# The first two chunks of a fused attention and MoE kernel done in halves of the inner dimension, and batches 0 and 1 in groups of four heads

## The chip, the cores and the metric

The kernel runs on one core of one Trainium2 chip. The metric is the device time in microseconds of one execution; the time before is the median of three runs. The engines are called TensorE (PE), VectorE (DVE), ScalarE (ACT), GpSimd (POOL) and SyncE (SP, whose queue issues every transfer).

## The reference

Sparse attention over 8 batches, 8 heads, 576 positions and head size 64, then a gated two-layer network on all 8 x 576 = 4608 tokens of width 512, with an inner width of 2048.

```python
# attention, per batch and head
scores = q @ k.T / sqrt(D)
rel = pos[:, None] - pos[None, :]
mask_local   = (rel >= 0) & (rel < 32)                       # heads 0 to 3
mask_strided = (rel >= 0) & (pos[None, :] % 32 == pos[:, None] % 32)   # heads 4 to 7
attn = softmax(where(mask, scores, -1e9));  attn_out = attn @ v
# network
x = attn_out.transpose(0, 2, 1, 3).reshape(4608, 512)
h = x @ w_in                                                 # 512 x 2048
g = h * erf(softplus(h))
out = g @ w_out                                              # 2048 x 512
```

## The kernel before

**Attention.** Both masks are nearly block diagonal. The host lays the data out so that a block of 96 queries meets 128 keys (local heads), and a block of 126 (seven residues modulo 32, 18 positions each) meets its own 126 keys (strided heads). A batch has three steps `j` for each kind; a step has two blocks, the last strided one a single block of 72. Heads are taken in pairs `hp`: 0 and 1 are local, 2 and 3 strided.

Batches 0 and 1 use `piece(b, hp, j, ...)`, one head pair each, twelve to a batch. Its steps: load `qk` and `v`; scores on PE (line 302), where the two heads' queries stand side by side with zeros in the other head's 64 rows, so that the full 128 rows are used; the mask added on PE (line 312) as a product with the identity; a copy to SBUF on ACT (`mask`, line 320); the maximum over the keys on POOL (`maxi`, line 328); its subtraction, on PE for batch 0 (line 332, by a negated identity) and on DVE for batch 1 (line 337); the exponential on ACT (line 341); the product with v on PE (line 345), where a column of ones gives the sum; reciprocal and scaling (lines 356 to 370); a transpose on PE (line 376); and the split of the result into a high and a low part, on ACT (`xhi`) and DVE (`xlo`, line 399).

Batches 2 to 7 use `quad(b, loc, j, ...)`: four heads at once, six to a batch. Its scores (line 502) are *tiled*: products of 64 rows by 64 columns on quarters of the array, and only over the queries that a half of the keys can meet. It masks by a minimum on DVE, sums on POOL, and needs no transpose.

**Network.** Tokens are done in chunks of 384 (`CH`), twelve of them; three chunks cover two batches. Every chunk runs over 16 blocks `f` of 128 inner columns; chunk `c` and block `f` make tile `k = 16 c + f`. In `ftile`, the first product (called mm1, line 725) takes 12 matmuls of 384 columns: high by high, low by high and high by low parts, each over four blocks of 128 input columns. Then a chain of ACT and DVE steps follows (the gate, four ACT activations and four DVE steps, with the split into `ghi` and `glo`). The second product (mm2, line 788) takes nine matmuls of 512 columns and adds into three PSUM banks `o0` to `o2`, which are held through the chunk's 16 blocks; at the last block ACT copies them out (line 803) and SP stores them (line 806). mm1s keep the order in which the chunks are listed.

**Weights.** They come as 64-bit floats: 32 loads of 512 KB, 16 of `w_in` (four input blocks for each 512 inner columns) and 16 of `w_out` (one for each block `f`). Each tile of words is turned into a 32-bit float by three DVE steps (lines 677, 684, 690), then split into a high part on ACT (line 695) and a low part on DVE (line 698). The float is held in a buffer of the tag `ob` in between. An mm1 needs its four `w_in` tiles, an mm2 its `w_out` tile.

**Order.** No engine's order is left to the program text. Each step is given to `Plan` with an engine, a duration, a key and what it comes after; `Plan.order` lists the steps by their estimated start and, among those that can start together, by key. The keys come from the constants at the top: `PRO + SLOT * k` for a tile, `W1K`, `W1S`, `W2K`, `W2S` for the weights, `A0K`, `A1K` and so on for the attention. SP's list goes by the same rule, with an estimate of the bytes still under way. Buffers (`bufs`) turn in order; a step that takes a buffer waits for the last users of it. While PE has nothing to do before the first mm1 it runs short products without use (`warm`, line 916).

```python
bufs = {"qk": 2, "v": 3, "sm": 3, "mx": 2, "tt": 2, "ps": 2, "h": 3, "a": 2, "ghi": 2, "glo": 2,
        "ob": 3, "r": 2}
```

Here `qk` and `v` are the loaded inputs, `sm` the scores in SBUF, `ps` and `h` PSUM banks (attention and mm1), `a`, `ghi`, `glo` the gate's values.

Of the kernel before, what the change touches and what calls it, by code (L numbers as in the profile page):

```python
# [1 line left out]

# [16 lines left out]
P = 128  # L19
# [9 lines left out]
PRO = 76.3437  # L29
SLOT = 5.25715  # L30
MM2 = 22.7481
W1K = (13.4993, 31.795, 47.8243, 102.53)
W1S = (0.491029, 16.2659, 6.41024, 9.24383)
W2K = 83.5416
W2S = 5.03476
A0K = 10.4625
A0S = 0.93245
A0D = -13.616
A1K = 82.9925
A1S = 4.98533  # L40
A1D = -10.6234
QE = (17.2927, 2.07406, 29.6184, 2.17352)
QO = (2.25354, 2.66589)
QD = (-0.95595, 4.13274, 3.34602, 4.05869, -2.26784)
ASH = 5.35876
ADT = -0.840127
BACKLOG = 0.566644
FT = (-0.468742, -1.24448, 5.36844, 0.898218, 4.98625, -0.907662, 1.11257, 2.41173, -0.633009)
# [5 lines left out]
WL = 2 * 2 * QL + 2 * QL + 32  # L54
WS = 2 * 2 * QS + 2 * P
# [141 lines left out]
def attention_moe(  # L197
# [16 lines left out]
    wpool = ctx.enter_context(tc.tile_pool(name="wpool", bufs=1))  # L214
    ps_a = ctx.enter_context(tc.tile_pool(name="ps_a", bufs=1, space=PSUM))
# [10 lines left out]
    cap = cpool.tile([P, SW], BF16, name="cap")[:, : 2 * QL + QS]  # L226
# [9 lines left out]
    pools = {"apool": apool, "mpool": mpool, "wpool": wpool, "ps_a": ps_a, "ps_h": ps_h, "ps_o": ps_o}  # L236
# [23 lines left out]
    def piece(b, hp, j, key, dt, ring, pe_mask=False, pool_sub=False, early=False):  # L260

        loc = hp < 2
        nblk = 1 if (not loc and j == 2) else 2
        n = QL if loc else (QS if j < 2 else S - 4 * QS)
        units, cols = 2 * nblk, 2 * nblk * n
        pid = f"{b}_{hp}_{j}"
        qk = buf("apool", "qk", [P, WS], f"qk_{pid}")  # L270
        v = buf("apool", "v", [P, 2, 2, D + 1], f"v_{pid}")
        s = buf("ps_h", "h", [P, 512], f"s_{pid}") if early else buf("ps_a", "ps", [P, 512], f"s_{pid}")
        sm = buf("apool", "sm", [P, 512], f"sm_{pid}")
        mx = buf("apool", "mx", [P, 512], f"mx_{pid}")
        pav = buf("ps_o", f"o{hp % 2}", [P, 512], f"av_{pid}") if early else buf("ps_a", "ps", [P, 512], f"av_{pid}")
        xn_b = buf("apool", "tt", [P, 512], f"xn_{pid}")
        xn = View(xn_b, "p (u d) -> p u d", slice(0, 4 * D), u=4)
        rc = buf("apool", "r", [P, 16, 1], f"r_{pid}")
        pt = buf("ps_a", "ps", [P, 512], f"t_{pid}")

        def load_qk():
            if loc:
                yield nc.sync.dma_start(qk[:, :WL], qk_loc[b, hp, j])
            else:
                w = nblk * (2 * n + P)
                yield nc.sync.dma_start(qk[:, :w], qk_str[b, hp - 2, j, :, :w])

        def load_v():
            w = nblk * 2 * (D + 1)
            yield nc.sync.dma_start(v.tile.rearrange("p b h d -> p (b h d)")[:, :w], v_all[b, hp, j, :, :w])  # L290

        def masks():
            if loc:
                m = mask_l if j == 0 else mask_l[:, 1:2]
                return m.broadcast_to([P, 2, 2, n]), "p (b h q) -> p b h q", dict(b=2, h=2)
            return mask_s[:, :, :n].broadcast_to([P, units, n]), "p (u q) -> p u q", dict(u=units)

        def scores():
            k0, step = units * n, n if loc else P
            for blk in range(nblk):  # L300
                dst = s[:, blk * 2 * n : (blk + 1) * 2 * n]
                yield nc.tensor.matmul(  # L302
                    dst,
                    qk[:, k0 + blk * step : k0 + blk * step + P],
                    qk[:, blk * 2 * n : (blk + 1) * 2 * n],
                    start=blk == 0,
                    stop=not pe_mask,
                    skip_group_check=True,
                )
                if pe_mask:  # L310
                    m = (mask_l[:, int(j > 0 or blk > 0)] if loc else mask_s[:, :, :n]).broadcast_to([P, 2, n])
                    yield nc.tensor.matmul(
                        dst.rearrange("p (h q) -> p h q", h=2), ident_b, m, start=False, stop=True,
                        skip_group_check=True,
                    )

        def mask():
            src, dst = s[:, :cols], sm[:, :cols]
            if pe_mask:
                yield nc.scalar.copy(dst, src)  # L320
            else:
                m, r, sizes = masks()
                yield nc.vector.tensor_tensor(
                    out=dst.rearrange(r, **sizes), in0=src.rearrange(r, **sizes), in1=m, op=ALU.add
                )

        def maxi():
            yield nc.gpsimd.partition_all_reduce(mx[:, :cols], sm[:, :cols], P, ReduceOp.max)  # L328
# [10 lines left out]
        def exp():  # L339
            d = sm[:, :cols]  # L340
            yield nc.scalar.activation(d, s[:, :cols] if early else d, AF.Exp, scale=1.0 / D**0.5)
# [680 lines left out]
```

## Time and profile before

| | |
|---|---|
| Median of three runs | 936.76 us (936.0 to 940.07) |
| The profiled execution | 934.98 us, span 933.2 us |
| PE busy | 921.7 us (99%) |
| DVE busy | 678.5 us (73%) |
| ACT busy | 576.7 us (62%) |
| POOL busy | 323.3 us (35%) |
| Moved by DMA | 68.83 MB, mean 74 GB/s |
| Granted PE clock | 1.000 |

PE's 99% holds the `warm` products too, and a matmul's record runs on beyond the start of the next, so a busy PE is not always one at full speed. What PE does usefully is read from the distance between the starts of its products. The shares of the other engines are means over a start in which DVE and the transfers are full and a long middle in which they are not.

### The profile page before, as it was taken

To read this page: it belongs to the slowest core of one execution; us is meant where nothing else is said; L and a number is where in the kernel's file an instruction comes from. 1 tells how busy PE (TensorE), PEld (TensorE's weight loads), DVE (VectorE), ACT (ScalarE), POOL (GpSimd) and SP (SyncE) were. 2 spreads that over 40 slices of the span, in tenths; PEclk is the share of its full clock that TensorE was granted. 3 is DMA by queue.
4 is the path that set the end of the run, shared out by engine and by line. 5 is a ranking of instruction groups with operands and counts; after the bars stand their busy time and mean duration, and the time that the engine had idled before them with its cause. 6 is when DMAs were issued, how large, how long until landed. Compare 5 with 4: busy or idle time off the path is not lost.

```text
span 933.2 us, 16156 instructions
## 1 busy us (share of the span) xinstructions
PE 921.7 (99%) x5993; PEld 813.2 (87%) x5993; DVE 678.5 (73%) x1539; ACT 576.7 (62%) x1283; POOL 323.3 (35%) x160
## 2 busy tenths in 40 slices
PE   7999999999999999999999999999999999999998
PEld 6888898888888888888888888889888888999997
DVE  6999998677777777766867777775777777555553
ACT  4776677556566656656656656655655666655654
POOL 3443104525263444513535543342525353000000
PEclk9999999999999999999999999999999999999999
DMA  8997202111212113102112111211211210000000
GB/s 286 310 317 255 60 22 80 39 46 59 78 51 80 43 54 100 46 12 78 59 48 92 60 48 52 80 39 35 91 47 50 80 48 4 34 1 0 34 1 35
DMA packets 37663, 68.83 MB, mean 74 GB/s; under 512 B 4176, under 2 KB 18640, under 8 KB 37584
## 3 DMA queue, kind: packets, MB, share of 16 engines
q1 hardware_dynamic: 37584, 67.80, 22.5%
q8 instruction: 47, 0.77, 0.4%
q14 instruction: 32, 0.26, 0.1%
HBM read 58.34 MB, written 9.44 MB: 73 GB/s over the span
## 4 chain that ended last, share of the span: by engine, by line
PE 92%; DVE 6%; DMA 1%; ACT 0%; issue 0%; SPq 0%
PE o L788 43%; PE h L725 41%; PE ps L592 3%; PE ps L502 2%; DVE w L684 1%; DVE w L690 1%; PE s L302 1%; DVE w L677 1%; DVE a L730 1%; DVE pair L698 1%; DMA qk<-qk_str 1%; DMA words<-w_in 1%; PE ps L490 0%; PE warm L916 0%; DVE xlo L399 0%; PE ps L302 0%
## 5 line engine op out<-in xcount | busy, mean ns | idle before, releaser
L788 PE MATMUL o<-pair,ghi 128*128 128x512 f32 x1152 | 364.5, 398 | 0.0
L733 ACT ACTIVATE a<-a 128x384 f32<-128x384 f32 x576 | 292.4, 522 | 95.5 <-DVE a L730 87.6
L730 DVE SCALAR_TENSOR_TENSOR a<-a,h 128x384 f32<-128x384 f32 x384 | 210.5, 549 | 163.9 <-ACT a L733 161.5
L725 PE MATMUL h<-xhi,pair 128*128 128x384 f32 x1536 | 299.5, 337 | 1.5 <-DVE glo L760 1.4
L725 PEld LDWEIGHTS h<-xhi,pair 128*128 128x128 f32 x1536 | 270.0, 188 | 10.7 <-DVE glo L760 2.7
L788 PEld LDWEIGHTS o<-pair,ghi 128*128 128x128 f32 x1152 | 209.4, 188 | 42.5 <-issue 1.5
L788 PE MATMUL o<-pair,glo 128*128 128x512 f32 x576 | 224.9, 390 | 0.0
L528 POOL PARTITION_ALL_REDUCE mx<-sm x66 | 100.1, 1560 | 352.1 <-DVE sm L520 343.3
L548 POOL PARTITION_ALL_REDUCE su<-sm x66 | 181.8, 2798 | 42.4 <-ACT sm L542 42.4
L733 ACT ACTIVATE a<-h 128x384 f32<-128x384 f32 x192 | 94.3, 491 | 141.4 <-PE h L725 140.5
L725 PE MATMUL h<-xlo,pair 128*128 128x384 f32 x768 | 164.5, 336 | 0.0
L754 DVE TENSOR_TENSOR h<-a,h 128x384 f32<-128x384 f32 x192 | 106.7, 556 | 42.3 <-ACT a L733 42.3
L725 PEld LDWEIGHTS h<-xlo,pair 128*128 128x128 f32 x768 | 135.9, 188 | 0.0
L788 PEld LDWEIGHTS o<-pair,glo 128*128 128x128 f32 x576 | 108.1, 188 | 23.6
L757 ACT CAST ghi<-h 128x384 fp32r<-128x384 f32 x192 | 90.8, 473 | 57.2 <-PE o L788 55.6
L760 DVE TENSOR_TENSOR glo<-h,ghi 128x384 fp32r<-128x384 f32 x192 | 105.2, 548 | 18.3 <-ACT ghi L757 15.3
L328 POOL PARTITION_ALL_REDUCE mx<-sm x24 | 41.5, 1734 | 63.1 <-ACT sm L320 56.8
L542 ACT ACTIVATE sm<-sm 128x384 f32<-128x384 f32 (+2 forms) x66 | 36.3, 554 | 18.6 <-DVE sm L535 17.6
L535 DVE TENSOR_TENSOR sm<-sm,mx 128x384 f32<-128x384 f32 (+2 forms) x66 | 39.8, 613 | 0.2
L520 DVE TENSOR_TENSOR sm<-ps,cap 128x384 f32<-128x384 f32 (+2 forms) x66 | 37.0, 585 | 0.0
L592 PEld LDWEIGHTS ps<-sm,v 128*64 128x64 f32 x528 | 24.6, 136 | 9.3 <-issue 6.5
L592 PE MATMUL ps<-sm,v 128*64 128x96 f32 (+2 forms) x528 | 31.7, 260 | 0.0
(59 smaller groups left out, 531.6 us busy)
## 6 DMA issues: line engine op xcount, KB each, us to landing
qk<-qk_loc SPq DMA_DIRECT2D x48, 304.0 KB, 3.3
qk<-qk_str SPq DMA_DIRECT2D x32, 380.0 KB, 3.6
v<-v_all SPq DMA_DIRECT2D x80, 130.0 KB, 2.2
out<-ob SPq DMA_DIRECT2D x36, 256.0 KB, 2.1
words<-w_in SPq DMA_DIRECT2D x16, 512.0 KB, 5.0
words<-w_out SPq DMA_DIRECT2D x16, 512.0 KB, 5.3
qk<-qk_str SPq DMA_DIRECT2D x16, 136.0 KB, 2.5
v<-v_all SPq DMA_DIRECT2D x16, 65.0 KB, 1.9
```

The lines of the kernel that those rows point to most:

```text
L328: yield nc.gpsimd.partition_all_reduce(mx[:, :cols], sm[:, :cols], P, ReduceOp.max)
L528: yield nc.gpsimd.partition_all_reduce(mx[k][:, :cols], sm[k][:, :cols], P, ReduceOp.max)
L535: yield nc.vector.tensor_tensor(out=d, in0=d, in1=mx[k][:, :cols], op=ALU.subtract)
L548: yield nc.gpsimd.partition_all_reduce(su[k][:, :cols], sm[k][:, :cols], P, ReduceOp.add)
L592: yield nc.tensor.matmul(px[h * D : (h + 1) * D, c0 : c0 + n], v[i][:, blk, h, :D], sm[bank][:, c : c + n], start=True, stop=True,)
L725: yield nc.tensor.matmul(ph[:, :CH], win[4 * s + cc][:, w, fs], x[cc][:, c0 : c0 + CH], start=(i == 0), stop=(i == len(terms) - 1))
L730: yield nc.vector.scalar_tensor_tensor(out=out, in0=in0, scalar=scalar, in1=in1, op0=op0, op1=op1)
L733: yield nc.scalar.activation(dst, src, func, bias=bias[i], scale=scale)
L754: yield nc.vector.tensor_tensor(out=ph[:, :CH], in0=a.tile, in1=ph[:, :CH], op=ALU.mult)
L757: yield nc.scalar.copy(ghi.tile, ph[:, :CH])
L760: yield nc.vector.tensor_tensor(out=glo.tile, in0=ph[:, :CH], in1=ghi.tile.bitcast(F32), op=ALU.subtract)
L788: yield nc.tensor.matmul(po.tile, g[:, ts], wout[f][:, w], start=(f == 0 and i == 0), stop=(f == NFC - 1 and i == 2),)
```

## The change

1. **Halves.** The list of chunks begins with chunk 0 over blocks 0 to 7, chunk 1 over blocks 0 to 7, chunk 0 over blocks 8 to 15, chunk 1 over blocks 8 to 15; from chunk 2 on it is as before. `ftile` gets a position `pos` in the list for its key, and the bounds `fs0` and `fs1` of its half. After a first half ACT copies the three banks out and SP stores them in DRAM (`keep`); before the end of the second half SP fetches them again (`fetch`, after all the `keep`s, the last weight and the joins of the chunk before), and DVE adds them to the banks (`join`) in place of ACT's copy.
2. **Groups.** `piece` is replaced by `head(b, loc, j, ...)`, four heads at once, six to a batch. Scores are tiled as in `quad`, with the mask still added on PE, once for each of two banks; each group's transposes go to one bank of `h`. The order within batches 0 and 1 is changed (`pairs`).
3. **Layout.** Both kinds of group now load all four heads by one transfer each for `qk` and `v`, and queries are stored without the zero halves (only the single block of 72 keeps them).
4. **Buffers and keys.** `v` 3 to 2 (of twice the size), `sm` 3 to 4, `ob` 3 to 2, `r` 2 to 3, `qk` 2 of twice the size. Every weight, every group of batches 0 and 1 and every quad has a key of its own.

```diff
-W1K = (13.4993, 31.795, 47.8243, 102.53)
-W1S = (0.491029, 16.2659, 6.41024, 9.24383)
-W2K = 83.5416
-W2S = 5.03476
+WK = (4.91144, 11.7736, 23.138, 24.5684, 81.8744, 38.4492, 69.5594, 67.3198, 63.8053, 87.1793, 23.8467, 61.9943, 34.3175, 127.093, 128.211, 116.829, 48.1787, 88.0229, 98.8806, 108.272, 109.35, 101.869, 119.148, 122.481, 143.689, 141.299, 147.526, 158.814, 180.44, 185.601, 167.447, 190.663)
+LD = (-3.85602, -21.1748, -3.28922)
+HK = (-0.530228, 7.20494, 8.53691, 33.1626, 35.9049, 38.4686, 41.9683, 60.4056, 62.9357, 79.7229, 107.532, 105.476)
...
-WL = 2 * 2 * QL + 2 * QL + 32
-WS = 2 * 2 * QS + 2 * P
+WL = 4 * QL + 32
+WS = 2 * QS + 2 * P
+WE = 2 * (S - 4 * QS) + P
...
-    bufs = {"qk": 2, "v": 3, "sm": 3, "mx": 2, "tt": 2, "ps": 2, "h": 3, "a": 2, "ghi": 2, "glo": 2,
-            "ob": 3, "r": 2}
+    bufs = {"qk": 2, "v": 2, "sm": 4, "mx": 2, "tt": 2, "ps": 2, "h": 3, "a": 2, "ghi": 2, "glo": 2,
+            "ob": 2, "r": 3}
...
+    def loads(g, key):
+        lq = plan.add("sp", P * 8 * g.wq / 3.6e5, key - LD[0], g.load_qk, new=[g.qk])
+        lv = plan.add("sp", P * 8 * g.wv / 3.6e5, key - LD[1], g.load_v, new=[g.v])
+        return lq, lv
+
+    def head(b, loc, j, key, dt, early, bank):
...
+        def scores():
+            yield from g.scores()
+            for k in range(nbank):
+                r, z, m = g.masks(k, mask_l, mask_s)
+                yield nc.tensor.matmul(
+                    s[k][:, :cols].rearrange(r, **z), ident_b, m, start=False, stop=True, skip_group_check=True
+                )
...
-            if f == NFC - 1:
-                ob = buf("mpool", "ob", [P, DM], f"ob{t}_{c}")
+            if f == fs1:
+                near = t == NTT - 1 and (c < 2 or c == NCHUNK - 1)
+                ob = buf("apool", "tt", [P, DM], f"ob{t}_{c}_{f}") if near else buf("mpool", "ob", [P, DM], f"ob{t}_{c}_{f}")
...
+                def join(po=po, ob=ob):
+                    yield nc.vector.tensor_tensor(out=ob.tile, in0=po.tile, in1=ob.tile, op=ALU.add)
...
+                if fs1 < NFC - 1:
+                    part[c, t] = buf("dpool", f"part{c}{t}", [P, DM], f"part{c}{t}")
+                    o = add("act", act(DM, 0.06), ke, evac, [o], [ob], [po])
+                    kept[c, t] = add("sp", d_io, ke + 0.1, keep, [o], [part[c, t]], [ob])
+                    continue
+                if fs0:
+                    o_f = add("sp", d_io, ke - PF, fetch, [*kept.values(), w2[-1], *joined[:c * NTT]], [ob], [part[c, t]])
+                    o = add("dve", dve(DM), ke, join, [o, o_f], [], [ob, po])
+                    joined.append(o)
...
+        if b == 1:
+            return [(True, 0), (False, 0), (False, 1), (False, 2), (True, 1), (True, 2)]
...
+        if b == 0:
+            return [(True, 0), (True, 1), (False, 0), (False, 1), (False, 2), (True, 2)]
...
+            if c < 2:
+                chunk(c, 0, NFC // 2)
+                if c == 1:
+                    chunk(0, NFC // 2, NFC)
+                    chunk(1, NFC // 2, NFC)
+            else:
+                chunk(c, 0, NFC)
```

More of the change, by code (lines that the diff above doesn't have):

```diff
@@ L1 @@
 from contextlib import ExitStack
+from types import SimpleNamespace
 import concourse.bass as bass
@@ new lines, in scores @@
+        def scores():
+            if nblk == 1:
+                for i in range(2):
+                    c = i * wq
+                    yield nc.tensor.matmul(
+                        s[0][:, 2 * i * n : 2 * (i + 1) * n], qk[:, c + 2 * n : c + 2 * n + P], qk[:, c : c + 2 * n],
+                        start=i == 0, stop=True, skip_group_check=True,
+                    )
+                return
+            used = set()
+            for i in range(2):
+                for blk in range(2):
+                    cq = i * wq + blk * n
+                    ck = i * wq + 2 * n + blk * (n if loc else P)
+                    for part in range(2):
+                        for h in range(2):
+                            rows, cols_k = slice(h * D, (h + 1) * D), slice(part * 64, (part + 1) * 64)
+                            bank, c = place(i, blk, h)
+                            q0, q1 = meet[part]
+                            yield nc.tensor.matmul(
+                                s[bank][cols_k, c + q0 : c + q1],
+                                qk[rows, ck + part * 64 : ck + (part + 1) * 64],
+                                qk[rows, cq + q0 : cq + q1],
+                                start=(bank, part) not in used,
+                                stop=True, skip_group_check=True,
+                            )
+                            used.add((bank, part))
@@ L701, in weight @@
         if wide:
-            op = add("sp", P * 8 * n / 3.6e5, key - 8.0, load, new=[words])
+            op = add("sp", P * 8 * n / 3.6e5, key - LD[2], load, new=[words])
             op = add("dve", dve(n, 0.5), key, bits0, [op], [w], [words])
@@ L789, in mm2 @@
                         po.tile, g[:, ts], wout[f][:, w],
-                        start=(f == 0 and i == 0), stop=(f == NFC - 1 and i == 2),
+                        start=(f == fs0 and i == 0), stop=(f == fs1 and i == 2),
                     )
             o = add(
-                "pe", 0.682, v0 + MM2 * SLOT + 0.2 * t, mm2, [o_l] + ready[1] + ([order_o[t]] if f else []),
-                [po] if f == 0 else [], [ghi, glo] + ([] if f == 0 else [po]),
+                "pe", 0.682, v0 + MM2 * SLOT + 0.2 * t, mm2, [o_l] + ready[1] + ([order_o[t]] if f > fs0 else []),
+                [po] if f == fs0 else [], [ghi, glo] + ([] if f == fs0 else [po]),
             )
@@ L854, in attention_moe @@
             rows, sl = slice(c * P, (c + 1) * P), slice(f, f + SW)
-            op, pair = weight(i, w_in, rows, sl, W1K[i // 4] + W1S[i // 4] * (i % 4))
+            op, pair = weight(i, w_in, rows, sl, WK[i])
             w1.append(op)
```

543 lines of the change are left out of this document (226 added, 317 removed).

## The prediction

> **What bounds the kernel now.** I read the page's slices first, then a table of stages, then TensorE's (PE's) own timeline, and last the chain that ended last. VectorE's (DVE's) row of the 40 slices (23.3 us each, tenths) shows that the first six slices are another kernel than the rest:
>
> ```profile
> DVE  6999998677777777766867777775777777555553
> ```
>
> The table of stages says it closer. Columns after the window: its length, then busy us and instructions of PE, PE's weight loads, DVE, ScalarE (ACT) and POOL, then PE's granted clock, DMA share, GB/s:
>
> ```profile
> 0.00:43.00 43.00, 37.99 (x262) 29.50 (x263) 32.68 (x79) 27.18 (x81) 19.72 (x16) 1.00 0.89 292
> 43.00:60.00 17.00, 15.57 (x101) 14.42 (x100) 17.00 (x38) 13.42 (x35) 3.60 (x3) 1.00 0.92 334
> 60.00:90.00 30.00, 29.25 (x181) 24.79 (x181) 29.85 (x75) 20.74 (x46) 12.93 (x6) 1.00 0.87 290
> 90.00:103.00 13.00, 12.38 (x71) 9.89 (x70) 13.00 (x30) 7.88 (x20) 4.22 (x3) 1.00 0.28 75
> 103.00:140.00 37.00, 37.00 (x226) 33.30 (x227) 37.00 (x81) 24.83 (x54) 1.25 (x1) 1.00 0.11 34
> 140.00:900.00 760.00, 760.00 (x5018) 675.40 (x5017) 535.09 (x1217) 465.91 (x1017) 281.62 (x132) 1.00 0.16 51
> ```
>
> From 103 us to the end PE has no gap, and its work there is fixed; time can only be won before. To 90 us the DMA stream runs near 300 GB/s, and from 43 to 140 us DVE is full. The fillers ("warm", line 916) have their own table of stages, first row below; PE's timeline gives the milestones (start, length, the wait in brackets):
>
> ```profile
> 0.00:50.00 50.00, 11.23 (x73) 1.00 0.90 303
> 42.88 1.64 PE L725 MATMUL h<-xhi,pair 128*128 128x384 f32 x8
> 48.00 0.49 PE L302 MATMUL ps<-qk 128*128 128x192 f32 x2
> 53.77 1.66 PE L725 MATMUL h<-xhi,pair 128*128 128x384 f32 x8 [1.40 <-DVE glo L760]
> 90.28 1.65 PE L725 MATMUL h<-xhi,pair 128*128 128x384 f32 x8
> 112.79 0.23 PE L376 MATMUL ps<-ident,xn 72*128 72x72 f32 x1
> ```
>
> The first MoE product (mm1 of tile 0) starts at T0 = 42.88; before it PE does batch 0 and 11.2 us of fillers. The ninth mm1 starts at T1 = 90.28, so eight tiles took 47.4 us. At full speed two tiles cost 4.17 + 4.08 us, by these chain rows:
>
> ```profile
> 190.69 4.17 PE h L725 x24
> 194.85 4.08 PE o L788 x18
> ```
>
> Eight tiles are 33 us at that rate, and not all their second products (mm2) were issued by T1. The rest is batch 1's attention on PE and stalls. Batch 1's scores begin at 48.00, its last transpose is at 112.79.
>
> **The change, part by part.**
>
> *Halves.* Chunk 0 runs hidden blocks 0 to 7, then chunk 1 the same, then chunk 0 and chunk 1 blocks 8 to 15. No matmul is added or dropped: 192 tiles stay. What moves is the deadline of 16 of the 32 weight tiles, by eight positions or more, and that of batch 1: chunk 1 now starts at position 8, not 16. A weight tile costs DVE four instructions:
>
> ```profile
> L684 DVE SCALAR_TENSOR_TENSOR w<-words,w 128x512 uint32<-128x512 uint32 x32 | 23.6, 737 | 0.1
> L690 DVE SCALAR_TENSOR_TENSOR w<-words,w 128x512 uint32<-128x512 uint32 x32 | 22.7, 710 | 0.1
> L698 DVE TENSOR_TENSOR pair<-w,pair 128x512 fp32r<-128x512 f32 x32 | 22.2, 695 | 0.4 <-ACT pair L695 0.2
> L677 DVE TENSOR_SCALAR w<-words 128x512 uint32<-128x512 uint32 x32 | 16.0, 503 | 5.0 <-DMA words<-w_in 5.0
> 60.83 0.60 DVE w L684
> 38.37 0.34 DVE w L677
> 53.71 0.47 DVE h L754
> ```
>
> The first four means sum to 2.64 us, but their records overlap; the chain's steps (0.34 and three of 0.60) sum to 2.14. I take 2.3, nearer the chain, because it counts no overlap. A MoE tile costs DVE four steps of 0.47, 1.9 us. Weights split (L698) and attention pieces split (L399, a piece being a head pair of a block) by 90 us:
>
> ```profile
> 0.00:90.00 90.00, 13.45 (x19) 1.00 0.89 299
> 0.00:90.00 90.00, 6.78 (x19) 1.00 0.89 299
> ```
>
> So 19 weights were ready, and 19 pieces: batch 0's twelve and seven of batch 1. The first eight tiles need 16 weights at most. Three spared give DVE 3 x 2.3 = 7 us; of batch 1 eight pieces are due (one local group, three strided), one more than was done. A piece has three long DVE steps, at 0.47 each 1.4 us. DVE alone would let the ninth mm1 go at 90.3 - 7 + 1.4 = 85, earlier by what T0 gains.
>
> The last weight is due when mm2 reaches it, about four tiles behind position 23, that is 20 positions after T1: 20 x 4.125 + 2 (PE's attention) = 84 us. DVE has to do in them sixteen weights (37 us), 20 tiles (38), batch 1's last four pieces (6) and three joins (2): 83. That just fits, so I charge 2 us of new stalls; bounds 0 (as in 103 to 140, where a full DVE stalled PE not at all) and 7 (three weights late).
>
> *Tiled scores in groups of four heads.* One head pair's scores and mask cost PE, from start to the next thing's start, 0.79 us (66.59 to 67.38, local) and 1.09 (62.22 to 63.31, strided):
>
> ```profile
> 62.22 0.69 PE L302 MATMUL ps<-qk 128*128 128x252 f32 x2
> 63.31 0.71 PE L788 MATMUL o<-pair,ghi 128*128 128x512 f32 x2
> 66.59 0.48 PE L302 MATMUL ps<-qk 128*128 128x192 f32 x2
> 66.91 0.24 PE L312 MATMUL ps<-con 128*128 128x192 bf16 x1
> 66.99 0.52 PE L302 MATMUL ps<-qk 128*128 128x192 f32 x2
> 67.38 1.65 PE L725 MATMUL h<-xhi,pair 128*128 128x384 f32 x8
> 113.02 1.44 PE o L788 x6
> 114.46 0.62 PE ps L502 x32
> ```
>
> Tiled, four heads cost 0.62 us (the quad's block), and masks of twice the width two times 0.16 (0.08 us for 192 columns, 66.91 to 66.99): 0.94 for 1.58 local, and with 0.2 a mask about 1.05 for 2.18 strided. Batch 1 saves 3 x 0.64 + 2 x 1.1 = 4.1 us; the one-block groups save nothing. PE is over 95% busy from 43 to 103, so I count 4; bounds 0 (DVE remains the limit) and 4.1. Batch 0's like saving lies beside fillers, so it counts only through T0.
>
> The Trainium skill, TensorEngine Tiling (Array Packing), section Key Properties, says that changing the tiling mode drains the engine. The row before the block is 1.44 us for six matmuls against 6 / 18 of 4.08 = 1.36, so this trace has at most 0.08 us for it; with twelve entries and exits at that price the saving would be about 2 us smaller over both batches.
>
> *Loads.* Queries are no longer stored with zero halves. The sizes before:
>
> ```profile
> qk<-qk_loc SPq DMA_DIRECT2D x48, 304.0 KB, 3.3
> qk<-qk_str SPq DMA_DIRECT2D x32, 380.0 KB, 3.6
> out<-ob SPq DMA_DIRECT2D x36, 256.0 KB, 2.1
> 27.89 0.33 SPq L286 DMA_DIRECT2D qk<-qk_str  x1
> 84.52 0.42 SPq L671 DMA_DIRECT2D words<-w_out  x1
> ```
>
> A local group falls from 608 to 416 KB, a strided one from 760 to 508: 1.08 MB a batch, 3.7 us of the stream at 292 GB/s. The last qk that chunk 0 needs was issued at 27.89; T0 came 15 us later, after mask, maximum, exponential, product, transpose and split. By the new keys there stand ahead of and in that load the constants (0.23 MB), two local and three strided qk (2.2), three v (0.8) and six weights of 128 x 512 x 8 bytes (3.1): 6.3 MB, 22 us of stream. Against it, a group of two banks takes longer from end to end, only two fit in four score copies, and the v loads come late in the keys. I take half to four fifths of the 6 us: T0 = 38, 5 us earlier; bounds 34 (all of it and shorter queues behind) and 44 (nothing, and a longer group).
>
> *Partial sums.* An evacuation at the end of the chain, and the nearest DVE step to a join:
>
> ```profile
> 929.51 0.58 ACT ob L803
> 529.90 0.68 DVE L535 TENSOR_TENSOR sm<-sm,mx 128x504 f32<-128x504 f32 x1
> ```
>
> Six more evacuations on ACT (0.58 us each), which is busy 24.8 of 37 us after 103; six stores and six fetches of 256 KB, 2.1 us to land, in a DMA at a quarter or less; six output copies become DVE adds, nearest a 0.68 us step on 504 columns, three of them counted above. PE: zero, as chunk boundaries cost no gap now; without that cover two boundaries of three evacuations, 3.5 us. The stores wait on ACT and the fetches on the last weight and the stores, with later loads queued behind them on SP. All weight loads were issued by 84.52, and batch 2 is first needed at position 48, so I cost the waits at zero; if a weight load were caught, its tile would be some 5 us late.
>
> *Quads.* Batches 2 to 7 keep their matmuls; one load replaces two and the staging has more room. PE is gap-free there: zero.
>
> **Sum.** T0 -5, scores -4, old stalls between 43 and 103 (2.8 us without work in the table) half gone -1, new DVE stalls +2: -8. The profiled execution took 934.98 us (span 933.2), 1.8 under the median of 936.76, so the median goes to 928.8; I say 928.5. With every term at its end the sum is -9 -4.1 -2 = -15 or +1 +7 = +8.
>
> **Rivals.** (a) *Batch 1 is late*, the one that ends slower. It must now be done in eight tiles, not sixteen. Its pieces came every 5.4 us (48 to 112.8 for twelve). Eight at that pace, plus the latency, set T1 at 91 to 97, and PE then has no other mm1 to run, since mm1s keep their order. The forecast has T1 near 83, so each us beyond adds one: from 91.3 on there is no gain, from 96 on it is 0.5% slower, and at 100 the median is 945. For it: DVE is full at this stage. Against: seven pieces were split by 90 us beside 19 weights, three of which can wait.
>
> (b) *DVE sets the pace anyway.* Weights and attention keep their DVE work, and the 83 us against 84 above turn into stalls of 7 instead of 2, while the scores bring nothing: 928.5 + 5 + 4 = 937.5, no change. For it: the 1.40 us wait on glo at 53.77 and full DVE to 140. Against: PE ran without gap from 103 to 140 beside a full DVE.
>
> (c) *The start is worth more.* T0 at 34, no new stall: -9 -4 -2 = 921.8. For it: 11.2 us of fillers before T0. Against: the chain of one group is long.
>
> **How the numbers follow.** Forecast (921 to 932) 0.53, (c) 0.16, (b) 0.18, (a) 0.13. A measurement tells about 0.5%, 4.7 us: below 932.1 is faster, above 941.4 slower. That gives 0.69, 0.18, 0.13. The range takes (c) with some more and (b): 917 to 938.
>
> **What would show it.** Right: first mm1 near 38 and ninth near 83; tiled score blocks near 0.62 us in the first 100 us; DVE full to 160 to 170 rather than 140; no wait of PE on DMA after 45; no gap at the half boundaries. Wrong: mm1 of position 8 waiting on xlo of batch 1, mm2 waiting on a weight pair between 110 and 170, mm1 or mm2 waiting on a join, or gaps past 200 us.

## The result, and the profile after

The changed kernel takes 945.47 us, against 936.88 for the kernel before on the same chip: a ratio of 1.0086, 95% interval [1.0065, 1.0106]. It is 0.9% slower; 928.5 was forecast, in 917 to 938. The 945.47 is the median of six executions, of which one was disturbed (1508.9 us at a granted clock of 0.558) and is left out of the ratio; the other five took 944.47 to 946.17, with a median of 945.18. The profile shown here is a second one of the same kernel, at 946.16 us.

> The changed kernel as it is, for a profile at full clock (its first profile was taken at a granted clock of 0.558, span 1507.1 us). Theory A (batch 1 is late): the ninth mm1 starts at 91 us or later, PE waits on xlo of batch 1, and the whole excess of about 8 us is lost before 110 us; past it PE is gap-free as before. Theory B (DVE sets the pace of the weights): the ninth mm1 starts near 83 to 86, and PE loses 7 to 17 us between 100 and 175, waiting on weight pairs or glo. Theory C (the loss is not in the start): first mm1 near 38, ninth near 83, and PE work or gaps beyond 200 us are 10 us or more above those of before.

The table of stages of the changed kernel, columns as before, and below it PE's timeline (first and ninth mm1 and one gap) and the groups of weights (L636) and attention pieces (L362, here half a group) split by 90 us:

```profile
0.00:43.00 43.00, 37.01 (x393) 27.84 (x394) 33.54 (x78) 26.25 (x78) 19.22 (x15) 1.00 0.94 336
43.00:60.00 17.00, 14.42 (x135) 12.10 (x134) 16.60 (x35) 12.58 (x33) 7.49 (x4) 0.90 0.97 366
60.00:90.00 30.00, 28.21 (x257) 23.68 (x257) 29.12 (x73) 20.20 (x47) 10.14 (x6) 1.00 0.52 182
90.00:103.00 13.00, 12.83 (x115) 11.37 (x114) 12.86 (x36) 7.36 (x18) 2.01 (x2) 1.00 0.19 52
103.00:140.00 37.00, 35.40 (x211) 31.77 (x210) 36.51 (x72) 25.84 (x56) 9.23 (x4) 1.00 0.13 45
140.00:900.00 760.00, 753.05 (x4939) 665.69 (x4938) 549.98 (x1217) 456.10 (x1001) 273.17 (x128) 1.00 0.14 45
```

```profile
42.02 1.65 PE L663 MATMUL h<-xhi,pair 128*128 128x384 f32 x8
55.69 0.55 PE L449 MATMUL t<-ident,xn 96*128 96x96 f32 x4 [2.54 <-DVE glo L698]
94.40 1.64 PE L663 MATMUL h<-xhi,pair 128*128 128x384 f32 x8
```

```profile
0.00:90.00 90.00, 13.11 (x19) 0.98 0.81 290
0.00:90.00 90.00, 5.77 (x18) 0.98 0.81 290
```

Three things are to be seen. The first mm1 came 0.86 us earlier, not 5. The ninth came 4.1 us later (94.40 for 90.28), with the same 19 weights split by 90 us as before: none was spared. And the long stage from 140 to 900, which had no gap, now lacks 6.95 us of PE, while DVE's time there grew from 535.1 to 550.0 us with the same number of instructions (1217).

How far the useful work has come can be counted: mm1 instructions by 4.17 / 24 us each, mm2 by 4.08 / 18, and 1.6 us for a quad's scores and products. In us of work done by a given time:

| done by | before | changed | even keys | one quad in, even keys | one quad in, own keys | whole chunks | halves alone |
|---|---|---|---|---|---|---|---|
| 100 us | 32.1 | 31.4 | 31.6 | 31.4 | 32.0 | 29.3 | 30.0 |
| 200 us | 129.1 | 127.1 | 128.7 | 128.1 | 129.1 | 120.5 | 123.2 |
| 400 us | 325.7 | 320.9 | 323.2 | 312.4 | 325.3 | 316.9 | 293.1 |
| 800 us | 721.0 | 709.0 | 713.9 | 707.0 | 715.4 | 706.9 | 687.5 |
| 400 to 800 | 395.3 | 388.1 | 390.7 | 394.6 | 390.1 | 390.0 | 394.4 |

(The other columns are experiments below.) So the changed kernel is 2 us behind at 200 us, and loses 10 more between 200 and 800, where nothing had been expected to change. The 2 us are one quad that is not done yet: of the network, both kernels have done the same by then (380 and 379 instructions of mm1, 252 of mm2). The table is of the profiled executions, whose spans differ by 11.2 us (944.4 and 933.2), more than the medians do. And PE's rows show only 4.3 of the 7 us lost between 400 and 800 as idle (395.74 busy of 400); where the other 3 lie is not shown. There are two questions: why the start gained nothing, and what the change did to the middle.

### The profile page after: what moved, and what is told of

Its sections match the earlier page's. It is cut to its first block, busy times and chain, and to the rows that moved or that the text cites. A ratio compares the mean times of both kernels' runs of the same rounds, so it can differ in the third digit from the quotient of the medians.

```text
span 1507.1 us, 16523 instructions
## 1 busy us (share of the span) xinstructions
PE 1498.4 (99%) x6238; PEld 1002.3 (67%) x6238; DVE 707.5 (47%) x1544; ACT 579.2 (38%) x1279; POOL 318.8 (21%) x158
## 2 busy tenths in 40 slices
DMA packets 25567, 63.14 MB, mean 42 GB/s; under 512 B 2832, under 2 KB 3984, under 8 KB 25488
## 4 chain that ended last, share of the span: by engine, by line
PE 99%; DMA 0%; ACT 0%; DVE 0%; issue 0%; SPq 0%
PE o L726 44%; PE h L663 44%; PE ps L552 3%; PE ps L310 2%; PE warm L875 1%; PE ps L414 1%; PE av L414 1%; PE ps L402 1%; PE t L449 0%; PE ps L295 0%; PE s L402 0%; PE ps L390 0%; DMA qk<-qk_loc 0%; PE s L310 0%; PE s L390 0%; PE s L295 0%
## 5 line engine op out<-in xcount | busy, mean ns | idle before, releaser
L726 PE MATMUL o<-pair,ghi 128*128 128x512 f32 x1152 | 553.4, 578 | 0.2 <-DVE pair L636 0.2
L663 PE MATMUL h<-xhi,pair 128*128 128x384 f32 x1536 | 480.4, 480 | 0.0
L663 PEld LDWEIGHTS h<-xhi,pair 128*128 128x128 f32 x1536 | 335.1, 220 | 123.5 <-issue 21.2
L726 PEld LDWEIGHTS o<-pair,ghi 128*128 128x128 f32 x1152 | 245.6, 217 | 168.1 <-issue 93.7
L726 PE MATMUL o<-pair,glo 128*128 128x512 f32 x576 | 329.7, 572 | 0.0
L663 PE MATMUL h<-xlo,pair 128*128 128x384 f32 x768 | 259.0, 480 | 0.0
L663 PEld LDWEIGHTS h<-xlo,pair 128*128 128x128 f32 x768 | 168.9, 220 | 52.7 <-issue 0.3
L726 PEld LDWEIGHTS o<-pair,glo 128*128 128x128 f32 x576 | 128.3, 223 | 88.0 <-issue 48.7
L552 PE MATMUL ps<-sm,v 128*64 128x96 f32 (+2 forms) x528 | 46.9, 346 | 0.0
L310 PEld LDWEIGHTS ps<-qk 64*64 64x64 f32 x1216 | 30.3, 182 | 22.0 <-issue 17.0
```

The lines of the kernel that those rows point to most:

```text
L310: yield nc.tensor.matmul(s[bank][cols_k, c + q0 : c + q1], qk[rows, ck + part * 64 : ck + (part + 1) * 64], qk[rows, cq + q0 : cq + q1], s ...
L552: yield nc.tensor.matmul(px[h * D : (h + 1) * D, c0 : c0 + n], g.vpart(i, blk, h, D), sm[bank][:, c : c + n], start=True, stop=True,)
L663: yield nc.tensor.matmul(ph[:, :CH], win[4 * s + cc][:, w, fs], x[cc][:, c0 : c0 + CH], start=(i == 0), stop=(i == len(terms) - 1))
L726: yield nc.tensor.matmul(po.tile, g[:, ts], wout[f][:, w], start=(f == fs0 and i == 0), stop=(f == fs1 and i == 2),)
```

## The experiments

The theory after the result: batches 2 to 7 lose in the middle because quads bunch and overlap, by their keys or by their staging; the rival is that the halves alone set batch 2 late and that this is the loss. All runs, with the median and the ratio to the kernel before on the same chip (two more were single profiles: the changed kernel again, 946.16, and even keys with both sets of old offsets again, 945.85):

| kernel | us | ratio, 95% interval |
|---|---|---|
| changed, even keys of quads | 942.59 | 1.0064 [1.0049, 1.0079] |
| before, changed kernel's keys of quads | 966.56 | 1.0320 [1.0305, 1.0336] |
| changed with whole chunks, even keys | 948.82 | 1.0131 [1.0115, 1.0146] |
| before with halves | 965.66 | 1.0305 [1.0288, 1.0322] |
| even keys, old offsets of quad and tile steps (three executions) | 947.84 | 1.0126 [1.0108, 1.0144] |
| even keys, three score buffers | 958.79 | 1.0244 [1.0227, 1.0261] |
| changed, eight weights later | 956.94 | 1.0226 [1.0208, 1.0244] |
| before, four score buffers | 938.03 | 1.0014 [1.0000, 1.0028] |
| even keys, quads on three score buffers | 950.81 | 1.0150 [1.0124, 1.0175] |
| changed, quads on three score buffers | 964.28 | 1.0296 [1.0270, 1.0321] |
| quads on three, batch 1 earlier, five weights later | 955.01 | 1.0193 [1.0165, 1.0221] |
| before, four score buffers, new offsets | 937.25 | 1.0004 [0.9993, 1.0015] |
| even keys, old offsets of quad steps | 949.25 | 1.0127 [1.0109, 1.0144] |
| before, batch 2 keyed later | 937.52 | 1.0001 [0.9992, 1.0011] |
| even keys, one quad in | 949.57 | 1.0148 [1.0132, 1.0163] |
| changed, one quad in | 940.91 | 1.0055 [1.0038, 1.0072] |

### Parts of the change by themselves

```diff
# even keys: the quads at the evenly spaced keys of the kernel before (slot and its constants come back too)
...
-                done = quad(b, loc, j, PRO + SLOT * GK[6 * b + i - 12], ADT * SLOT, ring)
+                done = quad(b, loc, j, PRO + SLOT * (slot + ASH), ADT * SLOT, ring)
# the reverse in the kernel before
-                done = quad(b, loc, j, PRO + SLOT * (slot + ASH), ADT * SLOT, ring)
+                done = quad(b, loc, j, 78.6727 + SLOT * GK[6 * b + i - 12], ADT * SLOT, ring)
```

> The changed kernel with one thing undone: the quads of batches 2 to 7 get the evenly spaced keys of the kernel before. Theory P (placement: the new keys put quads in bunches, where DVE and POOL fall behind and PE waits for glo): 934 to 937 us, PE without gaps from 200 to 900 us, DVE between 70 and 76% in each 100 us. Rival Q (room: the larger buffers let two quads run into each other whatever their keys): 942 or more, the POOL sums still coming 3 to 12 us apart. Rival R (the stores and fetches of the partial sums hold SP's queue and with it batch 2): at most 3 us won, 942 to 944, and the first quads still near 116, 133, 156 and then 211.

> The kernel before with one thing done: the quads get the keys that the changed kernel gives them. Theory P: slower by 5 to 10 us, 942 to 947, with waits of PE on glo between 200 and 800. Rival Q: no change, 936 to 938, since the small buffers hold one quad at a time. Rival R: no change either.

Even keys give back 2 to 3 of the 9 us, and the intervals of the two ratios overlap: the bunched keys are at most a part. The same keys cost the kernel before 30 us, and quads hardly overlap there (between 400 and 800 the two DVE steps looked at below take 589 and 204 ns).

```diff
# whole chunks in the changed kernel (even keys, weights' keys of before)
-                chunk(c, 0, NFC // 2)
...
+            chunk(c, 0, NFC)
# halves in the kernel before: second halves' weights 42 us later in the keys, batch 1 earlier and strided first
-A1K = 82.9925
+A1K = 62.0
...
+            if c < 2:
+                chunk(c, 0, NFC // 2)
...
```

> The groups of four heads alone: the changed kernel with whole chunks, the weights' keys of the kernel before and its evenly spaced keys of the quads. If the tiled scores and the smaller loads are worth what the prediction took (5 + 4 us): 926 to 930. If DVE's work before 140 us sets the pace whatever PE and DMA save: 935 to 938. If groups of four cost more than pairs: over 940.

> The halves alone: the kernel before with the first two chunks in halves, batch 1 put 21 us earlier in the keys with its strided heads first, and the weights of the second halves 42 us later. If the later deadlines of 16 weights are worth something by themselves: 928 to 933. If batch 1 in eight tiles takes back what the weights give: 935 to 938, ninth mm1 at 91 to 97. If the partial sums cost PE time: over 940, with waits at the half ends.

Neither part pays alone: groups without halves are 8.6 us behind at 200 us, halves without groups 5.9, both together 0.4 (even keys). The 400-to-800 row of the table parts them: whole chunks with the groups' staging lose 5.3 us there, halves with the old staging 0.9. So the loss of the middle belongs to the staging. Halves alone lose elsewhere, 16.6 us of PE between 300 and 400.

```diff
# even keys with the steps' offsets of before (QD and FT, which the change had moved too; and QD alone)
-QD = (2.01173, 6.12577, 5.8134, 5.43994, -1.80243)
+QD = (-0.95595, 4.13274, 3.34602, 4.05869, -2.26784)
```

> The kernel of x1_quadkeys with the offsets of the steps within a quad (QD) and within a tile (FT) of the kernel before, too; the four score buffers stay. Theory S (the offsets let a second quad begin before the first is through, so that POOL's sums stand between DVE's steps): 936 to 939 us, the subtraction on DVE back from 0.70 to 0.60 us, sums at even distances again. Rival Q (the fourth score buffer): 941 to 944, as x1_quadkeys.

> The kernel with evenly spaced quads and the older offsets of the quads' and the tile's steps (948.55 us, of which there is no undisturbed profile), for a profile. If the new offsets make the quads overlap: DVE's subtraction of 384 columns back near 0.60 us and the reciprocal's first step near 0.17 between 400 and 800, PE 399.5 us or more of 400; the 6 us by which it is longer than with the new offsets then lie in one stall before 400. If the overlap has another cause: 0.66 and 0.35, PE near 398.

> The changed kernel with evenly spaced quads and the older offsets of the quads' steps alone. If these offsets keep quads apart: subtraction of 384 columns near 0.60 us, reciprocal step near 0.17 between 400 and 800, PE 399.5 or more, and 937 to 940 us, unless a late batch 2 then stalls a change of chunk before 400 by 3 to 6 us (945). If they do not: as with the new offsets, 941 to 945.

With both sets of old offsets the subtraction of 384 columns is 719 ns and the reciprocal's first step 295, with the quads' alone 600 and 461, at 396.5 and 394.1 us of PE in 400: the overlap is there with old and new offsets. These offsets aren't the cause.

### Room for two quads

DVE's groups between 400 and 800 us tell overlap from none: the subtraction of the maximum (first row of each pair) and the first step of the reciprocal (second), before, changed, even keys, and even keys with one quad in; then the stage rows of the same four:

```profile
L535 DVE TENSOR_TENSOR sm<-sm,mx 128x384 f32<-128x384 f32 x20 | 11.4, 590 | 0.1
L574 DVE TENSOR_SCALAR r<-tt 128x12 f32<-128x12 f32 x10 | 1.7, 167 | 0.1
```

```profile
L334 DVE TENSOR_TENSOR sm<-sm,mx 128x384 f32<-128x384 f32 x22 | 16.4, 747 | 0.9 <-POOL mx L327 0.9
L534 DVE TENSOR_SCALAR r<-tt 128x12 f32<-128x12 f32 x11 | 6.3, 569 | 0.2
```

```profile
L337 DVE TENSOR_TENSOR sm<-sm,mx 128x384 f32<-128x384 f32 x20 | 13.0, 665 | 1.0 <-POOL mx L330 1.0
L537 DVE TENSOR_SCALAR r<-tt 128x12 f32<-128x12 f32 x10 | 3.5, 347 | 0.2
```

```profile
L338 DVE TENSOR_TENSOR sm<-sm,mx 128x384 f32<-128x384 f32 x20 | 10.9, 569 | 0.0
L538 DVE TENSOR_SCALAR r<-tt 128x12 f32<-128x12 f32 x11 | 1.8, 167 | 0.1
```

```profile
400.00:800.00 400.00, 400.00 (x2709) 354.41 (x2708) 290.39 (x677) 243.20 (x534) 162.53 (x77) 1.00 0.17 53
```

```profile
400.00:800.00 400.00, 395.74 (x2742) 347.43 (x2742) 299.06 (x673) 239.01 (x530) 169.55 (x80) 1.00 0.15 46
```

```profile
400.00:800.00 400.00, 397.90 (x2690) 348.98 (x2687) 296.32 (x678) 239.42 (x532) 165.69 (x78) 1.00 0.14 43
```

```profile
400.00:800.00 400.00, 400.00 (x2743) 353.47 (x2742) 294.24 (x690) 245.11 (x537) 171.80 (x80) 1.00 0.14 45
```

What the longer means consist of shows the changed kernel's timeline, POOL and DVE, around one gap of PE:

```profile
675.01 3.19 POOL L508 PARTITION_ALL_REDUCE su<-sm  x1 [2.13 <-ACT sm L341]
675.11 2.65 DVE L334 TENSOR_TENSOR sm<-sm,mx 128x504 f32<-128x504 f32 x1
677.95 0.54 DVE L698 TENSOR_TENSOR glo<-h,ghi 128x384 fp32r<-128x384 f32 x1
```

Behind it in the chain of waits:

```profile
678.54 2.36 PE h L663 x12
```

A subtraction that takes 0.68 us alone starts 0.1 us after POOL's sum and ends at 677.76, 0.44 before the sum's end. The split into `glo`, queued behind it on DVE, is 2 us late, and the chain runs through it to the next mm1. Another, at 663.27, behaves alike: 1.82 us, beside a sum from 663.00 to 665.51. The reciprocal's first step shows it most plainly: of the eleven in the changed kernel between 400 and 800, the seven that lie beside an instruction of POOL take 0.63 to 0.97 us, the four others 0.16 or 0.17; in the kernel before all ten lie beside none and take 0.16 or 0.17. Over the whole run PE waited 6.4 us in 11 places for `glo`, before 1.4 in one. The Trainium skill, SBUF — State Buffer, section Who interferes with whom, has the rule: an instruction of DVE with two SBUF inputs contends with one of GpSimd that reads SBUF, and the one that comes second is blocked. The two instances agree as to who waits; the wait is over before POOL's record is, since both subtractions ended some 0.4 us ahead of it. In the kernel before, quads come one after another, 16 to 20 us apart (the single blocks some 10), and the reciprocal's first step never meets POOL.

What lets them meet was looked for in four runs, and then in three more:

```diff
# score buffers: four in the kernel before; three in the changed one
-    bufs = {"qk": 2, "v": 3, "sm": 3, ...
+    bufs = {"qk": 2, "v": 3, "sm": 4, ...
# quads share three; only groups of batches 0 and 1 take a fourth
-"sm": 4,
+"sm": 3, "se": 1,
...
+        sm = [buf("apool", "se" if extra and i else "sm", ...) for i in range(nbank)]
```

> The kernel before with a fourth score buffer and nothing else. Theory Q: two quads run into each other and it is 2 to 6 us slower, 939 to 943, with longer subtractions on DVE. Theory S, or no theory of the buffers: 935 to 938.

> The kernel of x1_quadkeys with three score buffers instead of four, as before. Theory Q (the fourth buffer lets two quads run into each other): the part after 250 us is won back, 936 to 939, subtraction near 0.60 us; batch 0 may lose some us from groups that wait for buffers. Rival S (offsets of the steps): no gain, 941 to 946.

> The kernel of x1_quadkeys (evenly spaced keys of the quads) in which the quads share three score buffers and only the groups of batches 0 and 1 have a fourth. Theory Q2 (the loss after 200 us is two quads running into each other: DVE's subtraction and reciprocal step stand behind POOL's sum of the other quad): the first 200 us as x1_quadkeys, then at most 1 us lost from 400 to 800 us instead of 4.6; subtraction on 384 columns 0.60 to 0.62 us, reciprocal step 0.17; 936 to 939 in all. Rival (three buffers bring late quads at the chunk changes, as in x5_sm3 between 350 and 400): 943 or more with one long wait on xhi.

> The changed kernel, its own keys, with only the quads' fourth score buffer taken away. Theory Q2 with room alone as the cause: 936 to 940 and the DVE steps back at 0.60 and 0.17 us. Rival (the keys' bunches need the fourth buffer): the bunched quads wait for buffers, PE waits on xhi at chunk changes, 945 to 965 as when these keys were given to the kernel before.

A fourth score buffer in the kernel before does nothing (590 and 168 ns, PE 400.00). Three in the changed kernel bring its steps back: 612 and 170 ns with three for all, 618 and 170 with three for quads alone, each with 399.8 us of PE in 400. Yet both kernels are slower in all, since PE then stands still at a change of chunk instead (44.2 of 50 us between 350 and 400, clock 0.90, in the second). With the changed kernel's own keys three buffers for the quads stall it more: 964.28. Its steps are back too (569 and 176 ns), yet PE is busy for only 394.65 of the 400 us, less than with the overlap, because it now waits for quads (4.2 us in one place on `xhi`).

```diff
# before, four score buffers, and the changed kernel's offsets
+QD = (2.01173, 6.12577, 5.8134, 5.43994, -1.80243)
# a quad takes both input buffers, as a quad before did with its two transfers
+        q2 = [buf("apool", "qk", [P, 2 * WS], f"q2_{pid}")] if b > 1 else []
-        ... g.load_qk, new=[g.qk])
+        ... g.load_qk, new=[g.qk, *g.q2])
...
```

> The kernel before with four score buffers and the changed kernel's offsets of the quads' steps. If offsets and room together make quads overlap: subtractions of 384 columns at 0.65 us or more and the reciprocal's first step at 0.3 or more between 400 and 800, PE idle 2 us there, 941 to 945 us. If the loads by four heads or the halves are needed for it: 0.59, 0.17, PE 400.00, 936 to 939.

> The changed kernel with evenly spaced quads, in which each quad takes both input buffers, so that only one quad is loaded and scored at a time; nothing else differs from the run with evenly spaced quads (942.59 us). If the second input buffer lets quads overlap: DVE's subtraction of 384 columns at 0.60 us and the reciprocal's first step at 0.17 between 400 and 800, PE 399.5 us of 400, and with the start as it was some 937 to 939 us; with a stall at a change of chunk before 400 as with three score buffers, 945 to 951. If overlap has another cause: 0.66, 0.35, PE near 398, 942 to 945.

> The changed kernel with its own keys, in which each quad takes both input buffers. If the second buffer makes the overlap: subtraction of 384 columns at 0.60 to 0.62, reciprocal step at 0.17 to 0.2 between 400 and 800, PE 399 or more of 400; the keys of its quads, which lie in bunches, then stall PE elsewhere as they did with three score buffers (964) and in the kernel before (967): 950 to 967 us. If not: 0.75, 0.57, PE near 396, 945 to 948.

This is the part that was looked for. With four score buffers and the new offsets, but one quad in the inputs at a time, the kernel before stays at 570 and 166 ns and 937.25 us. The changed kernel with even keys goes back to 569 and 167 and PE to 400.00 of 400 by that one edit. So with even keys the overlap needs both: a second input buffer that holds a whole quad, and the fourth score buffer; take away either and it is gone. It doesn't make that kernel faster: 949.57, with one stall as with three score buffers:

```profile
350.00:400.00 50.00, 40.15 (x317) 34.61 (x315) 33.12 (x76) 24.72 (x57) 26.74 (x14) 0.90 0.22 68
```

```profile
PE ps L556 <- ACT sm L345: 6.4, 1, 6.4
PE h L667 <- ACT xhi L361: 2.9, 1, 2.9
```

With its own keys the edit gains instead: 940.91, the best of the changed kernels, 5.0 us above the kernel before on its chip instead of 8.6 (the intervals of the two ratios overlap a little). The prediction on record for it, 950 to 967, was wrong: the stall didn't come (50.00 of 50 between 350 and 400), and some overlap stayed (724 and 251 ns, PE 397.72 of 400). Not all of the gain is the overlap's: of the 6.4 us of work by which it is ahead of the changed kernel at 800 us, 2.0 were there at 200, 2.4 came between 200 and 400 and 2.0 after. It is still slower than before.

### Why quads are late: batch 2

With even keys quads that run one at a time stall PE in the changed kernel and not before, so something sets them late. The first test moved batch 2 in the kernel before:

```diff
+                late = (2.6, 5.2, 5.5, 3.9, 0.9, 0.0)[i] if b == 2 else 0.0
-                done = quad(b, loc, j, PRO + SLOT * (slot + ASH), ADT * SLOT, ring)
+                done = quad(b, loc, j, PRO + SLOT * (slot + late + ASH), ADT * SLOT, ring)
```

> The kernel before with the keys of batch 2's six quads 2.6, 5.2, 5.5, 3.9, 0.9 and 0 tiles later, which is by as much as the changed kernel writes them later. If a late batch 2 costs time by itself: PE gaps of 2 us or more before 420, 939 to 945 us. If there is room for it: 935.5 to 938, and the loss lies in how quads are staged.

It costs nothing, but it is a weaker test than was meant: its third to sixth quads wrote x only some 7 to 10 us later (the third at 208.78 for 201.44), where the kernel with even keys writes the third at 245.22 and the changed kernel at 230.11. What holds quads back is seen in the timelines. The halves do the first part. A quad may write x only behind the last mm1 of the chunks whose columns it overwrites (`ring` in the code), and halves move chunk 0's last mm1 from position 15, at 127.70 in the kernel before, to position 23. ACT's splits of the first two quads' x, both of chunk 0's columns, in the kernel before:

```profile
155.07 0.54 ACT L617 CAST xhi<-ps 128x192 fp32r<-128x192 f32 x2 [1.10 <-DVE ps L598]
172.81 0.54 ACT L617 CAST xhi<-ps 128x192 fp32r<-128x192 f32 x2
```

With even keys and one quad in, chunk 0's last mm1 on PE and the same splits:

```profile
164.60 1.55 PE L667 MATMUL h<-xhi,pair 128*128 128x384 f32 x8
165.99 0.86 PE L667 MATMUL h<-xlo,pair 128*128 128x384 f32 x4
167.27 0.54 ACT L361 CAST xhi<-ps 128x192 fp32r<-128x192 f32 x2
223.10 0.54 ACT L361 CAST xhi<-ps 128x192 fp32r<-128x192 f32 x2
```

With whole chunks and the groups' staging they start at 155.94 and 171.57, as before the change: it is the halves that make the first quad 12 us late and the second 50. What holds the second and those behind it shows the same kernel, with even keys and one quad in. There DVE turns a quad's sums (`tt<-su`) and joins partial sums (`ob<-o,ob`), POOL makes the sums (`su`), and SP fetches (`ob<-part`):

```profile
152.35 1.17 DVE L527 STREAM_TRANSPOSE tt<-su 64x384 f32<-64x384 f32 x2
158.58 5.01 POOL L512 PARTITION_ALL_REDUCE su<-sm  x2 [2.74 <-ACT sm L345]
182.45 1.46 SPq L759 DMA_DIRECT2D ob<-part  x3
213.16 1.87 DVE L750 TENSOR_TENSOR ob<-o,ob 128x512 f32<-128x512 f32 x3
218.51 0.56 DVE L527 STREAM_TRANSPOSE tt<-su 64x384 f32<-64x384 f32 x1
228.59 1.76 POOL L331 PARTITION_ALL_REDUCE mx<-sm  x1 [65.00 <-DVE sm L504]
```

The second quad's sums are there at 163.6, and are turned 55 us later; POOL stands 65 us. In the code the third output bank of the first two chunks takes its SBUF buffer from the tag `tt` (`near`, in `ftile`). There are two, and a quad needs both, for its turned sums and their reciprocals. With halves one is taken at each fetch and held through the half until the store has landed. In four kernels with halves and even keys, and in the kernel before with halves, the next turning starts 5.35 us behind the start of the second joins, wherever that lies: 212.80 and 218.15, 213.16 and 218.51, 216.12 and 221.47, 224.27 and 229.62, 218.53 and 223.88. In the other kernels with halves it is 4.9 to 6.2 us. With whole chunks sums are turned all through, at 166, 185, 199, 214 and 234.

The changed kernel's own keys evade most of this and meet another wait. They put first a quad of chunk 1's columns, which must not overwrite x before chunk 1's last mm1; its product is done by 151.2 and it writes at 199.95, holding one of two `ps` banks. ACT's and POOL's timeline:

```profile
199.95 0.32 ACT L357 CAST xhi<-ps 128x192 fp32r<-128x192 f32 x1 [0.62 <-PE h L663]
205.14 3.50 POOL L327 PARTITION_ALL_REDUCE mx<-sm  x2 [43.49 <-DVE sm L500]
225.36 2.51 POOL L508 PARTITION_ALL_REDUCE su<-sm  x1 [7.83 <-DVE tt L526]
```

The third quad's sums then wait for `tt` as well (join at 218.13, turned at 224.29). So batch 2 is held in both, with even keys by chunk 0's later end and then by the fetched sums, with the changed kernel's by the order and for 8 us by the fetched sums. A kernel with another buffer for the fetched sums was not tried, so their part rests on the coincidences and on the code. It would explain why room helps and hurts: late quads that go one at a time miss a chunk (the stalls between 350 and 400), and two at a time catch up with lengthened steps.

### The start

```diff
# eight w_in tiles of the second halves at keys 121 to 139 (from 24 to 128)
-WK = (..., 63.8053, 87.1793, 23.8467, 61.9943, 34.3175, 127.093, 128.211, 116.829, ...)
+WK = (..., 125.0, 127.0, 121.0, 123.0, 133.0, 135.0, 137.0, 139.0, ...)
# quads on three buffers; five w_in tiles at 108 to 118, and batch 1's groups earlier
-HK = (..., 41.9683, 60.4056, 62.9357, 79.7229, 107.532, 105.476)
+HK = (..., 41.9683, 52.0, 58.0, 66.0, 90.0, 96.0)
```

> The changed kernel with one thing done: the eight w_in tiles of the second halves get keys of 121 to 139, behind the start of position 8 (key 120.7); five of them stood at 24 to 87. Theory D (the halves gained nothing because DVE split 19 weights by 90 us as before, although 14 would do): the ninth mm1 goes 5 to 10 us earlier than 94.4, and the whole is 3 to 8 us faster than the changed kernel, 938 to 942. Rival L (the start hangs on the length of the chains of batch 1, not on DVE's load): ninth mm1 within 2 us of 94.4, 944 to 947. If the weights then come late: waits of PE on weight pairs between 120 and 170, 947 or more.

> The kernel of v1_quads3 with batch 1 earlier in the keys (52 to 96 in place of 60 to 107) and five w_in tiles of the second halves moved from 24 to 87 to 108 to 118. If DVE's order before position 8 is what held the start: ninth mm1 at 85 to 90 instead of 94, and 4 to 8 us faster than v1_quads3. If the chains of batch 1 hold it: ninth mm1 93 to 95 and no gain.

With the eight keyed later, 17 weights and not 19 are split by 90 us and 2.8 us more work is done by 100 us (34.2), but the ninth mm1 starts at 94.72, no earlier. Batch 1's last group for it is split at 91.95, as in the changed kernel at 92.54: whichever weights come first, it can't start before 92. That is not all that holds it: in the changed kernel PE starts the eighth mm1 only at 91.88 and goes from it to the ninth without a gap, and with the weights put off it runs twelve matmuls of mm2 between the two. By 200 us the put-off weights have cost 3.4 us (123.7). Batch 1 keyed earlier has 33.1 done by 100, and 120.5 by 200; its ninth mm1 starts at 95.19. Both bought early work with later stalls.

Where the first mm1's five microseconds went shows the last strided group that chunk 0 needs (72 of its keys), in the changed kernel, on SP and PE:

```profile
16.94 0.33 SPq L282 DMA_DIRECT2D qk<-qk_str  x1
25.73 1.81 PE L414 MATMUL av<-v,sm 128*126 128x65 f32 x15
27.38 0.71 PE L295 MATMUL s<-qk 128*128 128x144 f32 x4
34.03 0.70 PE L402 MATMUL s<-mx,neg 128*128 128x288 f32 x2
36.82 0.68 PE L414 MATMUL av<-v,sm 128*72 128x65 f32 x8
40.49 0.68 PE L449 MATMUL t<-ident,xn 72*128 72x72 f32 x2 [0.17 <-ACT xn L438]
```

And of the kernel before, its last piece of that kind:

```profile
32.43 0.41 PE L302 MATMUL s<-qk 128*128 128x144 f32 x2
40.83 0.28 PE L376 MATMUL ps<-ident,xn 72*128 72x72 f32 x1
```

The `qk` came 11 us earlier than before (16.94 for 27.89), more than forecast. The scores followed only at 27.38, right behind the product of the strided group two before it (25.73), whose score copies it takes over. That is still 5.05 us earlier than before. But the group needs 13.1 us from scores to transpose, the piece needed 8.4: 4.7 of the 5 are given back inside it.

## Why the prediction was wrong

**First mm1 at 38.** It came at 42.02: the term was 0.86 us and not 5. The transfers did shrink (63.14 MB for 68.83) and scores came 5 us earlier, but the longer group, which the prediction named and left at a fifth to a half of the gain, took nearly all.

**Scores, 4 us.** The price was near. A quad's block takes 0.62 us, as here in a chain of waits of the changed kernel; the five such blocks of batch 1 took 0.62, 0.63, 0.65, 0.82 and 1.02 us up to the start of their masks, the longest of them here on PE:

```profile
647.92 0.62 PE ps L310 x32
```

```profile
51.54 1.09 PE L310 MATMUL ps<-qk 64*64 64x72 f32 x32
52.56 0.60 PE L390 MATMUL ps<-con 128*128 128x504 bf16 x2
```

The saved time went idle: from 50 to 200 us PE lacked 6.9 us of work (45.64, 48.23 and 49.25 of 50 busy), before 2.8; in batch 0 it became fillers (14.5 us for 11.2). That is rival (b), DVE sets the pace anyway: with 4.1 us more idle than before where the forecast had 1 more (old stalls less 1, new ones 2), and scores worth nothing, it describes the start well.

**Three weights spared.** The step took the later deadline for a later key. By 90 us 19 were split as before, so the ninth mm1 came at 94.40, inside the 91 to 97 of rival (a). Its price, one for each us beyond 83, held roughly: 928.5 + 11.4 is 940, and work done at 200 us stands 2 us behind the kernel before. When weights did move, batch 1 still kept the ninth mm1 behind 92, as rival (a) had said, though it alone does not explain 94.40.

**"Quads: zero", and the waits of stores and fetches at zero.** These two steps failed outright; between 200 and 800 us the profiled execution lost 10 us where zero was put. "One load replaces two and the staging has more room" was the very thing: more room let quads overlap, and DVE's steps lengthened beside POOL's instructions (747 and 569 ns for 590 and 167). That part is shown; with one quad in at a time the changed kernel lost 2.3 us of PE between 400 and 800 instead of 4.3. The cost of halves was sought on SP and PE, while what they do is end chunk 0 eight positions later and, by the code and the coincidences above, hold a buffer that batch 2 needs. Of the signs listed as wrong, "gaps past 200 us" is the one that came; no mm1 or mm2 waited on a join.

That DVE would be full to 160 to 170 was nearly so: 49.51 of 50 us between 100 and 150, then 35.41.

**What stays open.** What overlap and lateness cost each: they could not be taken away together with the same keys. Every key was kept or moved by hand, and the keys of one arrangement cost another up to 30 us, so the sums of single parts don't add up.

## What to carry to other kernels

A buffer count is also a schedule: one more buffer can let two chains overlap that had been kept apart, and what then meets on another engine must be costed, not only what is saved. When a step takes its buffer from a tag, ask who else turns in that tag and for how long it is held; here a fetched sum holds one for 30 us. A deadline that moves frees nothing until the order moves with it.

## What the runs showed of the hardware

The same gap of 2.54 us on PE was followed by a lower clock in some profiles and not in others: of the seven kernels that have it near 55 us, four show a granted clock of 0.54 to 0.72 in the 3 us from 55 to 58, and three 1.00. The rows from 55 to 58 us, changed kernel and the same with one quad in, whose start is the same but for small shifts (its gap ended at 54.58):

```profile
55.00:58.00 3.00, 2.31 (x9) 1.92 (x10) 2.97 (x7) 2.39 (x7) 2.31 (x2) 0.72 0.99 371
```

```profile
55.00:58.00 3.00, 3.00 (x21) 2.49 (x19) 2.97 (x7) 1.87 (x6) 2.30 (x2) 1.00 1.04 422
```

Three matmuls of an mm2 took 1.28 us there (57.19 to 58.47) instead of 0.69; it cost some 1.7 us. The Trainium skill, TensorE: Matmul & The Clock Gate, section What's actually happening, speaks of windows of about 3.4 us that run on freely, and its table lets the clock fall after an idle one. A clock that falls behind a gap of 2.54 us is more than that table says; that it falls in some profiles and not in others agrees with windows that run on freely.

DVE's `TENSOR_SCALAR` with one SBUF input (the reciprocal's first step) also lengthened beside POOL, from 0.16 or 0.17 us alone to 0.63 to 0.97; one of 0.73 us, at 670.43, lies beside two of POOL's maxima that run from 669.38 to 672.88. It does not always: with even keys two of the five that lie beside POOL took 0.17.
